# Decode attention on one core: the output projection's weights as one last transfer, and K transposed in double chunks

## Chip, cores, metric

One core of a Trainium2 chip. The metric is the device time of one execution in microseconds (us), median of several runs. All runs that are compared here agree within some tenths of a per cent and count as fast runs. (e6_alone below ran once, so its state is unknown; only its trace is used. A difference under 2% counts as "the same" on record; smaller differences are called real here where the 95% interval excludes 1.)

## The reference

One decode step: attention of 2 batches with 32 heads over a cache of 16384 positions, mixed by a gate with a small MLP.

```python
q = (x @ wq)                                  # 2 x 32 heads x 128
scores = einsum("bhqd,bhkd->bhqk", q, k_cache) * 128 ** -0.5
p = softmax(scores); o = einsum("bhqk,bhkd->bhqd", p, v_cache)
a = o.reshape(B, 1, 32 * 128) @ wo            # wo: 4096 x 1024, bf16, 8.4 MB
b = mlp(B_x)                                  # w1, w2, w3, w4
out = g * a + (1 - g) * b
```

K and V are 537 MB of the 572.5 MB that are read once. Everything else has to hide behind that stream.

## The kernel before

K and V come as 64 tiles of 8.4 MB (two heads of one batch each) into a ring of three buffers; one partition of a tile is a contiguous run of 64 KB. K is transposed on the vector engine in 32x32 blocks, 512 elements at a time. The wo rows come head by head: one transfer of 256 KB per head, 2 KB runs (row `h*128+d` on partition `d`), used by 8 matmuls as soon as that head is finished in both batches.

```python
SLOT = NJ * Dh          # 64 KB a partition; three such buffers
V_SPLIT_LAST = [NJ // 2, NJ // 4, NJ // 8, NJ // 16, NJ // 16]   # last V in five pieces

def load_wo(h):
    t = ...             # [P, D], own small ring
    nc.sync.dma_start(out=t[:], in_=A_wo[h * Dh : (h + 1) * Dh, :])

def qk_stage(i):
    ...
    for m in range(NM):                       # 16
        for wh in range(2):
            T = t_tile([P, CJ, 32], FP32)     # 512 elements a partition
            nc.vector.transpose(out=T[:], in_=Kw[:, m * CJ : (m + 1) * CJ, wh, :])
            ...                               # two matmuls on T into S

def pv_stage(i):
    ...
    (pv_rows if i < NT - 1 else pv_cols)(V, PT, oc)
    nc.vector.tensor_tensor(out=OT[:, hg * G : (hg + 1) * G, b], in0=oc[:], in1=rinv[:], op=ALU.mult)

def wo_stage(h):        # OT: [d, head, batch]
    woh = wo_tiles.pop(h)[:].rearrange("d (p c) -> d p c", c=KC)
    for c in range(KC):
        nc.tensor.matmul(wo_acc[:, c, :], lhsT=woh[:, :, c], rhs=OT[:, h, :], ...)
# ... the transfers and stages are issued in the order k0, k1, v0, k2, v1, o0, ...
```

Of the kernel before, what the change touches and what calls it, by code (L numbers as in the profile page):

```python
# [10 lines left out]
FP32 = mybir.dt.float32  # L11
BF16 = mybir.dt.bfloat16
ACTF = mybir.ActivationFunctionType
ALU = mybir.AluOpType
# [9 lines left out]
def kernel(  # L24
# [17 lines left out]
    B, Sq, D = A_x.shape  # L42
    _, H, Sk, Dh = A_k_cache.shape
    F = B_w3.shape[1]
    assert Sq == 1 and Dh == P and B == 2 and H % 2 == 0
    G = 2
    NJ = G * Sk // P
    CJ = 16
# [11 lines left out]
    const = ctx.enter_context(tc.tile_pool(name="const", bufs=1))  # L60
    big = ctx.enter_context(tc.tile_pool(name="big", bufs=NBIG))
    tpool = ctx.enter_context(tc.tile_pool(name="tpool", bufs=2))
    wpool = ctx.enter_context(tc.tile_pool(name="wpool", bufs=1))
    ppool = ctx.enter_context(tc.tile_pool(name="ppool", bufs=1))
    stat = ctx.enter_context(tc.tile_pool(name="stat", bufs=2))
    sps = ctx.enter_context(tc.tile_pool(name="sps", bufs=2, space=PSUM))
# [7 lines left out]
    def big_tile(name):  # L74
        return big.tile([P, SLOT], BF16, tag="big", name=name)

    def t_tile(shape, dtype, name="T"):
        return tpool.tile(shape, dtype, tag="T", name=name)
# [3 lines left out]
    tiles = [(b, hg) for hg in range(NHG) for b in range(B)]  # L82
    kn_tiles = {}
    vn_tiles = {}
    wo_tiles = {}
    wt = {}
    V_SPLIT_LAST = [NJ // 2, NJ // 4, NJ // 8, NJ // 16, NJ // 16]

    def cache_rows(cache, i):
        b, hg = tiles[i]  # L90
        return cache[b, hg * G : (hg + 1) * G].rearrange("a s d -> (a s) d").rearrange(
            "(p j) d -> p j d", p=P
        )
# [7 lines left out]

    def load_v(i):
        t = big_tile("Vn")
        tv = t[:].rearrange("p (j d) -> p j d", d=Dh)
        src = cache_rows(A_v_cache, i)
        j0 = 0
        for n in V_SPLIT_LAST if i == NT - 1 else [NJ]:
            nc.sync.dma_start(out=tv[:, j0 : j0 + n, :], in_=src[:, j0 : j0 + n, :])
            j0 += n
        vn_tiles[i] = t  # L110

    def load_rows(keys, srcs):
# [7 lines left out]
            wt[key] = v  # L120
            c0 += R * N

    def load_wo(h):
        if h >= H - G:
            t = t_tile([P, D], BF16, "woh")
        else:
            t = wpool.tile([P, D], BF16, tag="woh", name="woh")
        nc.sync.dma_start(out=t[:], in_=A_wo[h * Dh : (h + 1) * Dh, :])
        wo_tiles[h] = t


    x_pm = const.tile([P, B, KC], BF16)
# [55 lines left out]
    for a in range(4):  # L188
        nc.vector.memset(own[32 * a : 32 * a + 32, 2 * a : 2 * a + 2], 1.0)
    ZW = P + NM  # L190
    NZ = 2
    z_tiles = []
    for n in range(NZ):
        z = const.tile([P, 4, ZW], BF16, name=f"z{n}")
# [76 lines left out]
        )  # L271


    OT = const.tile([P, H, B], BF16)
    wo_acc = acc.tile([P, KC, B], FP32, name="wo_acc")
    S_tiles = {}
    PT_tiles = {}
    rs_tiles = {}

    def qk_stage(i):  # L280
        Kw = kn_tiles.pop(i)[:].bitcast(FP32).rearrange("p (j w e) -> p j w e", w=2, e=32)
        z = z_tiles[i % NZ]
        S = sps.tile([P, NC_], FP32, name="S")
        S_tiles[i] = S
        for m in range(NM):
            for wh in range(2):
                T = t_tile([P, CJ, 32], FP32)
                nc.vector.transpose(out=T[:], in_=Kw[:, m * CJ : (m + 1) * CJ, wh, :])  # L288
                Tb = T[:].rearrange("p j s -> p (j s)").bitcast(BF16).rearrange(
                    "p (n two) -> p n two", two=2  # L290
                )
                for par in range(2):
                    nc.tensor.matmul(  # L293
                        S[:],
                        lhsT=z[:, 2 * wh + par, NM - 1 - m : NM - 1 - m + P],
                        rhs=Tb[:, :, par],
                        start=(m == 0 and wh == 0 and par == 0),
                        stop=(m == NM - 1 and wh == 1 and par == 1),
                    )

    def softmax_stage(i):
        S = S_tiles.pop(i)
# [26 lines left out]
    def pv_rows(V, PT, oc):  # L329



        O = ops.tile([P, 4 * Dh], FP32, name="O")
        for m in range(NM):
            for g in range(4):
                j0 = m * CJ + 4 * g
                nc.tensor.matmul(  # L337
                    O[32 * g : 32 * g + 32, :],
                    lhsT=PT[:, m : CJ * 32 : 16],
                    rhs=V[:, j0 : j0 + 4, :],  # L340
                    start=(m == 0),
                    stop=(m == NM - 1),
                )
        Os = ppool.tile([P, 4, Dh], FP32, tag="PrOs", name="Os")
        nc.scalar.copy(out=Os[:].rearrange("p x d -> p (x d)"), in_=O[:])  # L345
        for x in range(4):
            nc.tensor.matmul(  # L347
                oc[:], lhsT=Os[:, x, :], rhs=osel[:, x, :], start=(x == 0), stop=(x == 3)
            )

    def pv_cols(V, PT, oc):
        for j in range(NJ):
            c = (j % CJ) * 32 + j // CJ
            nc.tensor.matmul(  # L354
                oc[:],
                lhsT=V[:, j, :],
                rhs=PT[:, c : c + 17 : 16],
                start=(j == 0),
                stop=(j == NJ - 1),
            )  # L360

    def pv_stage(i):
        b, hg = tiles[i]
        PT = PT_tiles.pop(i)
        rs = rs_tiles.pop(i)
        V = vn_tiles.pop(i)[:].rearrange("p (j d) -> p j d", d=Dh)
        rs2 = stat.tile([P, G], FP32, name="rs2")
        nc.vector.tensor_scalar(
            out=rs2[:], in0=hmask[:], scalar1=rs[:, 0:1], scalar2=None, op0=ALU.mult
        )  # L370
        rinv = stat.tile([P, G], FP32, name="rinv")
        nc.vector.reciprocal(out=rinv[:], in_=total(rs2[:])[:])
        oc = misc_psum([P, G])
        (pv_rows if i < NT - 1 else pv_cols)(V, PT, oc)
        nc.vector.tensor_tensor(  # L375
            out=OT[:, hg * G : (hg + 1) * G, b], in0=oc[:], in1=rinv[:], op=ALU.mult
        )

    def wo_stage(h):

        woh = wo_tiles.pop(h)[:].rearrange("d (p c) -> d p c", c=KC)
        for c in range(KC):
            nc.tensor.matmul(  # L383
                wo_acc[:, c, :],
                lhsT=woh[:, :, c],
                rhs=OT[:, h, :],
                start=(h == 0 and c == 0),
                stop=(h == H - 1 and c == KC - 1),
            )


    def layernorm(src, dst):
# [20 lines left out]
        nc.vector.tensor_tensor(out=dst, in0=cen[:], in1=over_r(rstd[:]), op=ALU.mult)  # L413

    def gelu(pre_f32, dst_bf, C):
        sq = const.tile([P, C, B], FP32, name=f"gelu_sq{C}")
        nc.vector.tensor_tensor(out=sq[:], in0=pre_f32, in1=pre_f32, op=ALU.mult)
        nc.vector.tensor_scalar(
            out=sq[:], in0=sq[:], scalar1=GELU_C1, scalar2=1.0, op0=ALU.mult, op1=ALU.add
        )  # L420
        nc.vector.tensor_tensor(out=sq[:], in0=sq[:], in1=pre_f32, op=ALU.mult)
        nc.scalar.activation(out=sq[:], in_=sq[:], func=ACTF.Tanh, scale=GELU_C0)
        nc.vector.tensor_scalar(
            out=sq[:], in0=sq[:], scalar1=1.0, scalar2=0.5, op0=ALU.add, op1=ALU.mult
        )
        nc.vector.tensor_tensor(out=dst_bf, in0=sq[:], in1=pre_f32, op=ALU.mult)

    def linear(key, actT):

        w = wt.pop(key)  # L430
        R, C = w.shape[1], w.shape[2] // P
        ps = misc_psum([P, C, B])
        for c in range(C):
            for r in range(R):
                nc.tensor.matmul(  # L435
                    ps[:, c, :],
                    lhsT=w[:, r, :].rearrange("k (p c) -> k p c", c=C)[:, :, c],
                    rhs=actT[:, r, :],
                    start=(r == 0),
                    stop=(r == R - 1),  # L440
                )
        return ps
# [3 lines left out]
    shT = const.tile([P, KC, B], BF16)  # L446
    x1 = const.tile([P, KC, B], FP32)
    xn2T = const.tile([P, KC, B], BF16)
    h2 = const.tile([P, FC, B], FP32)
    h2T = const.tile([P, FC, B], BF16)  # L450
    pre = const.tile([P, KC, B], FP32)

# [11 lines left out]
        layernorm(x1[:], xn2T[:])  # L464

    def st_up():
        nc.vector.tensor_copy(out=h2[:], in_=linear("w3", xn2T)[:])
        gelu(h2[:], h2T[:], FC)

# [14 lines left out]
    for i in range(-1, NT):  # L484
        if i + 1 < NT:
            xfers.append(("big", f"k{i + 1}", lambda i=i: load_k(i + 1)))
            steps.append((f"k{i + 1}", lambda i=i: (build_z(i + 1), qk_stage(i + 1))))
        if i >= 0:
            xfers.append(("big", f"v{i}", lambda i=i: load_v(i)))
            steps.append((f"v{i}", lambda i=i: pv_stage(i)))  # L490

            for h in range(max(i - 1, 0), i + (i == NT - 1)) if i else ():
                ring = "wo" if h < H - G else "T"
                xfers.append((ring, f"o{h}", lambda h=h: load_wo(h)))
                steps.append((f"o{h}", lambda h=h: wo_stage(h)))
        if i + 1 < NT:
            steps.append(("", lambda i=i: softmax_stage(i + 1)))
        if i in extra:
            xfers.append(("big", f"x{i}", extra[i][0]))
            steps.append((f"x{i}", extra[i][1]))  # L500

    ring_size = {"big": NBIG, "wo": 1, "T": G}
    ring_used = {"big": [], "wo": [], "T": [f"k{NT - 1}"] * G}
    done = set()

    def issue_ready():
# [54 lines left out]
```

## Time and profile before

| | before |
|---|---|
| time, median of 4 runs | 1350.89 us |
| share of the load queue | 98.7% of 16 DMA engines |
| PE / vector engine (DVE) busy | 68% / 58% |
| last packet of loads ends | 1345.0 us |

These are lines of the page of before: the span, the busy times, two rows of the span in 40 slices (DMA is the busy share of 16 DMA engines in tenths, GB/s what they moved), the queues, and two groups of instructions (busy us, mean ns of one, idle time before them and what ended it).

```profile
span 1349.4 us, 14402 instructions
...
PE 918.6 (68%) x5770; PEld 402.5 (30%) x5770; DVE 786.5 (58%) x1373; ACT 45.0 (3%) x99; POOL 14.3 (1%) x45
...
DMA  9999999999999999999999999999999999999995
GB/s 405 436 436 434 430 432 428 434 430 428 436 423 436 440 427 424 435 441 428 424 440 434 430 426 436 429 429 440 428 428 440 430 426 419 426 422 438 435 418 220
...
q1 hardware_dynamic: 15808, 572.54, 98.7%
...
q14 instruction: 22, 0.18, 0.0%
...
L288 DVE STREAM_TRANSPOSE T<-Kn 128x512 f32<-128x512 f32 x1024 | 691.3, 702 | 231.3 <-DMA Kn<-in_A_k_cache_dram 164.7
...
L383 PE MATMUL wo_acc<-OT,woh 128*128 128x2 bf16 x256 | 20.1, 200 | 4.0 <-DVE OT L375 4.0
```

The DMA row says it all: full until the last slice. The vector engine's 231 us of idle time before its transposes were mostly ended by a K tile that arrived, so it waits for DMA and not the other way round.

The timeline of before at its end (start, length, engine, line, operation, tile, count, idle before):

```profile
1344.82 0.17 DVE L375 TENSOR_TENSOR OT<-misc,rinv 128x2 bf16<-128x2 f32 x1 [6.75 <-PE misc L354]
1344.90 1.21 PEld L383 LDWEIGHTS <-woh 128*128 128x128 bf16 x16 [0.21 <-DMA woh<-in_A_wo_dram]
1345.04 1.16 PE L383 MATMUL wo_acc<-OT,woh 128*128 128x2 bf16 x16 [0.26 <-DVE OT L375]
1346.23 0.17 DVE L524 TENSOR_TENSOR fin<-wo_acc,g_bc 128x16 f32<-128x16 f32 x1 [1.25 <-PE wo_acc L383]
```

The last V product is done at 1344.8 and the last packet of wo ends at 1345.0; 4.4 us after that the kernel is over. There is little to gain at the end other than by ending the stream earlier.

In the records a transfer is a set of packets, here one for each contiguous run: the 8192 packets of 64 KB are 64 tiles of 128 partitions, the 4096 of 2 KB are 32 heads of 128 rows. The records of single DMA packets are in the trace too. They are not on the page; these are sums over them.

```
packet of   count   usual length
64 KB        8192   2.42 us    (27 GB/s for one engine)
 2 KB        4096   0.084 us   (24 GB/s: the wo rows)
```

### The profile page before, as it was taken

To read this page: it belongs to the slowest core of one execution; us is meant where nothing else is said; L and a number is where in the kernel's file an instruction comes from. 1 tells how busy PE (TensorE), PEld (TensorE's weight loads), DVE (VectorE), ACT (ScalarE), POOL (GpSimd) and SP (SyncE) were. 2 spreads that over 40 slices of the span, in tenths; PEclk is the share of its full clock that TensorE was granted. 3 is DMA by queue.
4 is the path that set the end of the run, shared out by engine and by line. 5 is a ranking of instruction groups with operands and counts; after the bars stand their busy time and mean duration, and the time that the engine had idled before them with its cause. 6 is when DMAs were issued, how large, how long until landed. Compare 5 with 4: busy or idle time off the path is not lost.

```text
span 1349.4 us, 14402 instructions
## 1 busy us (share of the span) xinstructions
PE 918.6 (68%) x5770; PEld 402.5 (30%) x5770; DVE 786.5 (58%) x1373; ACT 45.0 (3%) x99; POOL 14.3 (1%) x45
## 2 busy tenths in 40 slices
PE   2677766677667766667766776666876666776667
PEld 2132322432225322223222532222322222332224
DVE  0677765467553655556665365555766555666554
ACT  0000000000000000000000000000000000000000
POOL 0000000000000000000000000000000000000000
PEclk9988878798777777789877787788987778997777
DMA  9999999999999999999999999999999999999995
GB/s 405 436 436 434 430 432 428 434 430 428 436 423 436 440 427 424 435 441 428 424 440 434 430 426 436 429 429 440 428 428 440 430 426 419 426 422 438 435 418 220
DMA packets 15875, 573.46 MB, mean 425 GB/s; under 512 B 2368, under 2 KB 2368, under 8 KB 6720
## 3 DMA queue, kind: packets, MB, share of 16 engines
q1 hardware_dynamic: 15808, 572.54, 98.7%
q8 instruction: 45, 0.74, 0.2%
q14 instruction: 22, 0.18, 0.0%
HBM read 572.53 MB, written 0.00 MB: 424 GB/s over the span
## 4 chain that ended last, share of the span: by engine, by line
DMA 49%; PE 27%; DVE 18%; issue 2%; another core or an unknown queue 2%; ACT 1%; SPq 0%; ACTq 0%
DMA Kn<-in_A_k_cache_dram 49%; PE S L293 19%; DVE T L288 17%; PE O L337 5%; PE misc L347 1%; PE misc L203 1%; PE wo_acc L383 1%; ACT Os L345 1%; PE misc L354 1%; ACT Pr L321 0%; DVE PT L325 0%; DVE mx L314 0%; DVE OT L375 0%; DVE nb L316 0%
## 5 line engine op out<-in xcount | busy, mean ns | idle before, releaser
L288 DVE STREAM_TRANSPOSE T<-Kn 128x512 f32<-128x512 f32 x1024 | 691.3, 702 | 231.3 <-DMA Kn<-in_A_k_cache_dram 164.7
L293 PE MATMUL S<-T,z_133 128*128 128x512 bf16 x1024 | 334.3, 420 | 145.0 <-DVE T L288 133.5
L293 PE MATMUL S<-T,z_135 128*128 128x512 bf16 x1024 | 336.3, 423 | 139.4 <-DVE T L288 124.0
L293 PEld LDWEIGHTS <-z_133 128*128 128x128 bf16 x1024 | 106.7, 104 | 369.8 <-issue 316.1
L293 PEld LDWEIGHTS <-z_135 128*128 128x128 bf16 x1024 | 107.2, 105 | 365.1 <-issue 312.2
L337 PE MATMUL O<-Vn,PT 128*32 128x512 bf16 x1984 | 114.1, 383 | 0.0
L375 DVE TENSOR_TENSOR OT<-misc,rinv 128x2 bf16<-128x2 f32 x32 | 5.2, 163 | 151.4 <-PE misc L347 144.6
L337 PEld LDWEIGHTS <-PT 128*32 128x32 bf16 x1984 | 71.1, 140 | 42.7 <-issue 13.7
L345 ACT COPY Os<-O 128x512 f32<-128x512 f32 x31 | 18.1, 585 | 1099.8 <-PE O L337 1099.8
L347 PE MATMUL misc<-osel,Os 128*128 128x2 f32 x248 | 32.7, 254 | 12.6 <-ACT Os L345 11.1
L435 PEld LDWEIGHTS <-wt 128*128 128x128 bf16 x576 | 35.8, 172 | 16.0 <-DMA wt<-in_B_w_dram 14.7
L325 DVE STREAM_TRANSPOSE PT<-Pr 128x512 bf16<-128x512 bf16 x32 | 22.7, 711 | 28.7 <-ACT Pr L321 28.7
L347 PEld LDWEIGHTS misc<-osel,Os 128*128 128x128 f32 x248 | 30.0, 191 | 21.1 <-ACT Os L345 21.1
L304 DVE TENSOR_REDUCE m<-S 128x1 f32<-128x512 f32 x32 | 22.2, 692 | 22.5 <-PE S L293 22.5
L314 DVE TENSOR_REDUCE mx<-misc 64x1 f32<-64x64 f32 x64 | 14.2, 222 | 23.9 <-PE misc L203 23.5
L321 ACT ACTIVATE Pr<-S,nb 128x512 bf16<-128x512 f32 x32 | 22.0, 687 | 131.0 <-DVE nb L316 128.0
L241 PE MATMUL misc<-xT,wt 128*128 128x2 bf16 x256 | 7.1, 165 | 25.8 <-DVE xT L236 22.9
L383 PEld LDWEIGHTS <-woh 128*128 128x128 bf16 x256 | 20.7, 168 | 10.4 <-issue 10.2
L383 PE MATMUL wo_acc<-OT,woh 128*128 128x2 bf16 x256 | 20.1, 200 | 4.0 <-DVE OT L375 4.0
L203 PE MATMUL misc<-mdiag,ones_f 128*128 128x128 f32 x64 | 16.7, 347 | 8.5 <-DVE mdiag L307 8.5
L435 PE MATMUL misc<-xn2T,wt 128*128 128x2 bf16 x224 | 14.4, 202 | 7.3 <-DMA wt<-in_B_w_dram 7.3
L435 PE MATMUL misc<-h2T,wt 128*128 128x2 bf16 x224 | 13.6, 199 | 7.0 <-DMA wt<-in_B_w_dram 7.0
(173 smaller groups left out, 140.0 us busy)
## 6 DMA issues: line engine op xcount, KB each, us to landing
wt<-in_B_w_dram SPq DMA_DIRECT2D x2, 7168.0 KB, 46.9
woh<-in_A_wo_dram SPq DMA_DIRECT2D x32, 256.0 KB, 30.1
wt<-in_B_w_dram SPq DMA_DIRECT2D x2, 2048.0 KB, 36.4
Vn<-in_A_v_cache_dram SPq DMA_DIRECT2D x1, 4096.0 KB, 38.9
Vn<-in_A_v_cache_dram SPq DMA_DIRECT2D x1, 2048.0 KB, 43.3
Vn<-in_A_v_cache_dram SPq DMA_DIRECT2D x1, 1024.0 KB, 45.2
Vn<-in_A_v_cache_dram SPq DMA_DIRECT2D x2, 512.0 KB, 46.9
Kn<-in_A_k_cache_dram SPq DMA_DIRECT2D x32, 48.9
```

Of the source, the lines that this page charges most:

```text
L203: nc.tensor.matmul(ps[:], lhsT=ones_f[:], rhs=src, start=True, stop=True)
L288: nc.vector.transpose(out=T[:], in_=Kw[:, m * CJ : (m + 1) * CJ, wh, :])
L293: nc.tensor.matmul(S[:], lhsT=z[:, 2 * wh + par, NM - 1 - m : NM - 1 - m + P], rhs=Tb[:, :, par], start=(m == 0 and wh == 0 and par == 0), ...
L304: nc.vector.reduce_max(out=m[:], in_=S[:], axis=AX.X)
L314: nc.vector.reduce_max(out=mx[pa, :], in_=mall[pa, pa], axis=AX.X)
L321: nc.scalar.activation(out=Pr[:], in_=S[:], func=ACTF.Exp, bias=nb[:], scale=scale, accum_out=rs[:])
L325: nc.vector.transpose(out=PT[:], in_=Pr[:])
L337: nc.tensor.matmul(O[32 * g : 32 * g + 32, :], lhsT=PT[:, m : CJ * 32 : 16], rhs=V[:, j0 : j0 + 4, :], start=(m == 0), stop=(m == NM - 1),)
L345: nc.scalar.copy(out=Os[:].rearrange("p x d -> p (x d)"), in_=O[:])
L347: nc.tensor.matmul(oc[:], lhsT=Os[:, x, :], rhs=osel[:, x, :], start=(x == 0), stop=(x == 3))
L383: nc.tensor.matmul(wo_acc[:, c, :], lhsT=woh[:, :, c], rhs=OT[:, h, :], start=(h == 0 and c == 0), stop=(h == H - 1 and c == KC - 1),)
L435: nc.tensor.matmul(ps[:, c, :], lhsT=w[:, r, :].rearrange("k (p c) -> k p c", c=C)[:, :, c], rhs=actT[:, r, :], start=(r == 0), stop=(r == ...
```

## The change

Intent: read wo in long runs instead of 2 KB, without small transfers between the K and V tiles, and spend fewer vector instructions on K. After the last V, wo comes as one transfer into a big buffer, in six pieces of 16, 8, 4, 2, 1, 1 rows a partition. Partition `32a+h` gets rows `h*128 + 32a + r`, r = 0..31, a contiguous 64 KB. That is the order in which one transpose of 32x32 blocks puts the head outputs. To make room, one z tile goes, and some small tiles move into the ring of T.

```diff
-    V_SPLIT_LAST = [NJ // 2, NJ // 4, NJ // 8, NJ // 16, NJ // 16]      # last V now whole, by rows
-    def load_wo(h): ...
+    WO_SPLIT = [16, 8, 4, 2, 1, 1]
+    def load_wo():
+        t = big_tile("wo")[:].rearrange("p (r n) -> p r n", n=D)
+        src = A_wo.rearrange("(h a r) n -> a h r n", a=4, r=32)
+        r0 = 0
+        for n in WO_SPLIT:
+            nc.sync.dma_start(out=t[:, r0 : r0 + n, :], in_=src[:, :, r0 : r0 + n, :])
+            r0 += n
 ...
-    NZ = 2
+    NZ = 1
 ...  # qk_stage: one transpose of [P, 2, CJ, 32] (1024 elements) and four matmuls, 16 times a tile
+            T = t_tile([P, 2, CJ, 32], FP32)
 ...
-    def wo_stage(h): ...
+    def wo_stage():
+        Q = const.tile([P, B, 32], BF16)
+        for b in range(B):
+            nc.vector.transpose(out=Q[:, b, :], in_=OT[:, b, :])     # OT: [d, batch, head]
+        wo = wt.pop("wo").rearrange("k r (p c) -> k r p c", c=KC)
+        for r in range(32):
+            for c in range(KC):
+                nc.tensor.matmul(wo_acc[:, c, :], lhsT=wo[:, r, :, c], rhs=Q[:, :, r], ...)
 ...
+    xfers.append(("big", "wo", load_wo)); steps.append(("wo", wo_stage))
```

More of the change, by code (lines that the diff above doesn't have):

```diff
@@ L44 @@
     F = B_w3.shape[1]
-    assert Sq == 1 and Dh == P and B == 2 and H % 2 == 0
+    assert Sq == 1 and Dh == P and B == 2 and H == 32
     G = 2
@@ L62 @@
     tpool = ctx.enter_context(tc.tile_pool(name="tpool", bufs=2))
-    wpool = ctx.enter_context(tc.tile_pool(name="wpool", bufs=1))
     ppool = ctx.enter_context(tc.tile_pool(name="ppool", bufs=1))
@@ L84 @@
     vn_tiles = {}
-    wo_tiles = {}
     wt = {}
-    V_SPLIT_LAST = [NJ // 2, NJ // 4, NJ // 8, NJ // 16, NJ // 16]
     def cache_rows(cache, i):
@@ L103, in load_v @@
         t = big_tile("Vn")
-        tv = t[:].rearrange("p (j d) -> p j d", d=Dh)
-        src = cache_rows(A_v_cache, i)
-        j0 = 0
-        for n in V_SPLIT_LAST if i == NT - 1 else [NJ]:
-            nc.sync.dma_start(out=tv[:, j0 : j0 + n, :], in_=src[:, j0 : j0 + n, :])
-            j0 += n
+        nc.sync.dma_start(
+            out=t[:].rearrange("p (j d) -> p j d", d=Dh), in_=cache_rows(A_v_cache, i)
+        )
         vn_tiles[i] = t
@@ L121, in load_rows @@
             c0 += R * N
-    def load_wo(h):
-        if h >= H - G:
-            t = t_tile([P, D], BF16, "woh")
-        else:
-            t = wpool.tile([P, D], BF16, tag="woh", name="woh")
-        nc.sync.dma_start(out=t[:], in_=A_wo[h * Dh : (h + 1) * Dh, :])
-        wo_tiles[h] = t
+    WO_SPLIT = [16, 8, 4, 2, 1, 1]
[6 more added lines that the diff above has]
+            r0 += n
+        wt["wo"] = t
     x_pm = const.tile([P, B, KC], BF16)
@@ L271, in build_z @@
         )
-    OT = const.tile([P, H, B], BF16)
+    OT = const.tile([P, B, H], BF16)
     wo_acc = acc.tile([P, KC, B], FP32, name="wo_acc")
@@ L280, in qk_stage @@
     def qk_stage(i):
-        Kw = kn_tiles.pop(i)[:].bitcast(FP32).rearrange("p (j w e) -> p j w e", w=2, e=32)
+        Kw = kn_tiles.pop(i)[:].bitcast(FP32)
         z = z_tiles[i % NZ]
@@ L284, in qk_stage @@
         S_tiles[i] = S
+        CW = CJ * Dh // 2
         for m in range(NM):
-            for wh in range(2):
-                T = t_tile([P, CJ, 32], FP32)
-                nc.vector.transpose(out=T[:], in_=Kw[:, m * CJ : (m + 1) * CJ, wh, :])
-                Tb = T[:].rearrange("p j s -> p (j s)").bitcast(BF16).rearrange(
-                    "p (n two) -> p n two", two=2
-                )
-                for par in range(2):
-                    nc.tensor.matmul(
-                        S[:],
-                        lhsT=z[:, 2 * wh + par, NM - 1 - m : NM - 1 - m + P],
-                        rhs=Tb[:, :, par],
-                        start=(m == 0 and wh == 0 and par == 0),
-                        stop=(m == NM - 1 and wh == 1 and par == 1),
-                    )
+            T = t_tile([P, 2, CJ, 32], FP32)
+            nc.vector.transpose(
+                out=T[:].rearrange("p w j s -> p j w s"),
+                in_=Kw[:, m * CW : (m + 1) * CW].rearrange("p (j w e) -> p j w e", w=2, e=32),
+            )
+            Tb = T[:].rearrange("p w j s -> p w (j s)").bitcast(BF16).rearrange(
+                "p w (n two) -> p w n two", two=2
+            )
+            for v in range(4):
+                nc.tensor.matmul(
+                    S[:],
+                    lhsT=z[:, v, NM - 1 - m : NM - 1 - m + P],
+                    rhs=Tb[:, v // 2, :, v % 2],
+                    start=(m == 0 and v == 0),
+                    stop=(m == NM - 1 and v == 3),
+                )
     def softmax_stage(i):
@@ L349, in pv_rows @@
             )
-    def pv_cols(V, PT, oc):
-        for j in range(NJ):
-            c = (j % CJ) * 32 + j // CJ
-            nc.tensor.matmul(
-                oc[:],
-                lhsT=V[:, j, :],
-                rhs=PT[:, c : c + 17 : 16],
-                start=(j == 0),
-                stop=(j == NJ - 1),
-            )
     def pv_stage(i):
@@ L373, in pv_stage @@
         oc = misc_psum([P, G])
-        (pv_rows if i < NT - 1 else pv_cols)(V, PT, oc)
+        pv_rows(V, PT, oc)
         nc.vector.tensor_tensor(
-            out=OT[:, hg * G : (hg + 1) * G, b], in0=oc[:], in1=rinv[:], op=ALU.mult
+            out=OT[:, b, hg * G : (hg + 1) * G], in0=oc[:], in1=rinv[:], op=ALU.mult
         )
-    def wo_stage(h):
-        woh = wo_tiles.pop(h)[:].rearrange("d (p c) -> d p c", c=KC)
-        for c in range(KC):
-            nc.tensor.matmul(
-                wo_acc[:, c, :],
-                lhsT=woh[:, :, c],
-                rhs=OT[:, h, :],
-                start=(h == 0 and c == 0),
-                stop=(h == H - 1 and c == KC - 1),
-            )
+    def wo_stage():
[5 more added lines that the diff above has]
+            for c in range(KC):
+                nc.tensor.matmul(
+                    wo_acc[:, c, :],
+                    lhsT=wo[:, r, :, c],
+                    rhs=Q[:, :, r],
+                    start=(r == 0 and c == 0),
+                    stop=(r == 31 and c == KC - 1),
+                )
     def layernorm(src, dst):
@@ L415, in gelu @@
     def gelu(pre_f32, dst_bf, C):
-        sq = const.tile([P, C, B], FP32, name=f"gelu_sq{C}")
+        sq = t_tile([P, C, B], FP32, "gelu")
         nc.vector.tensor_tensor(out=sq[:], in0=pre_f32, in1=pre_f32, op=ALU.mult)
@@ L448 @@
     xn2T = const.tile([P, KC, B], BF16)
-    h2 = const.tile([P, FC, B], FP32)
     h2T = const.tile([P, FC, B], BF16)
@@ L466, in st_up @@
     def st_up():
+        h2 = t_tile([P, FC, B], FP32, "h2")
         nc.vector.tensor_copy(out=h2[:], in_=linear("w3", xn2T)[:])
@@ L490 @@
             steps.append((f"v{i}", lambda i=i: pv_stage(i)))
-            for h in range(max(i - 1, 0), i + (i == NT - 1)) if i else ():
-                ring = "wo" if h < H - G else "T"
-                xfers.append((ring, f"o{h}", lambda h=h: load_wo(h)))
-                steps.append((f"o{h}", lambda h=h: wo_stage(h)))
         if i + 1 < NT:
@@ L500 @@
             steps.append((f"x{i}", extra[i][1]))
-    ring_size = {"big": NBIG, "wo": 1, "T": G}
-    ring_used = {"big": [], "wo": [], "T": [f"k{NT - 1}"] * G}
+    xfers.append(("big", "wo", load_wo))
+    steps.append(("wo", wo_stage))
+    ring_size = {"big": NBIG}
+    ring_used = {"big": []}
     done = set()
```

## The prediction

> **What bounds the kernel now.** DMA. The queue table gives the load queue 98.7% of 16 engines' span; PE is 68% and DVE 58% busy (page). In the packet records of the trace the last load packet ends 1345.0 us after the span's start; 4.4 us remain (16 matmuls, two DVE operations, the store). Most engines end at 1330 to 1336 us, two at 1343 and 1345. K's work is off the path: DVE waits 5.8 us for the last K tile (chain of waits).
>
> **Removed.**
> - 32 transfers of 256 KB in 2 KB packets. A 2 KB packet takes 84 ns, a 64 KB one 2420 (packet records): 21.8 us of all 16 engines for wo, against an estimated 19.7 in the new runs (32 KB 1215 ns, 16 KB 613, 8 KB 309, 4 KB 159, 2 KB 84). About 2 us, on the path.
> - 512 transposes' fixed cost. 702 ns for 512 elements is about 0.53 us of elements and 0.17 fixed (my split), so 1.24 us for a double chunk instead of 1.40: 85 us less DVE time, worth nothing under a DMA limit.
> - The last V tile's 256 column matmuls (6.9 us, timeline) become rows (3.6 us).
>
> **Added or moved.**
> - All 256 wo matmuls stand at the end, 63 ns each as in the first projection (64 in 3.96 us): 16 us. If wo landed at full rate, PE would end about 6 us behind the last piece, and the time would be about 1353 us.
> - The new transfer's source is 4 blocks, then 32 heads, then a contiguous run; the two outer strides cannot merge, so the slowest dimension is 4. [...] The trace of before has no such transfer to check it. If it holds, 8.4 MB go through 4 engines: 32 partitions x 2.46 us = 79 us (estimate from the packet times above) instead of 20.
>
> **Sum.** Without wo ahead of it, each engine ends V 22 us earlier: most at 1308 to 1313 us, the late two at 1320 to 1323. The wo transfer waits for the last K tile, done at about 1304, so it is queued by then. Plus 79: 1387 to 1392, or up to 1402 if a late engine is among the four. Plus 3.9 of tail and 1.5 between span and timed run: 1393 to 1407. I say 1398 us, range 1386 to 1411. If all 16 engines work, 1348 to 1356.
> Chances: faster by over 2% 0.01, within 2% 0.21, slower 0.78.
>
> **What would show it.** The last two slices at a quarter DMA share and about 108 GB/s; the chain of waits ending in wo transfers; wo pieces landing some 39, 20, 10, 5 us apart; 2 KB packets down from 4096 to 256; 512 transposes at 1.2 to 1.25 us. With 16 engines: wo lands 20 us after V, then 5 to 6 us of matmuls.
>
> **What would make it wrong.** The lowering splits the dimension, or spreading follows partitions, so that 16 engines work; four engines alone exceed 27 GB/s each; the single z buffer starves the queue, which I do not expect.

"If it holds" refers to the premise that the new transfer, with a slowest dimension of 4, runs on four engines. The result shows that it did (a DMA share of 0.25, four reports of landing a piece). 1308 to 1323 for the end of V, plus 79 for wo on four engines, plus 3.9 and 1.5, came to 1393 to 1407, and the prediction said 1398. The 79 us are an estimate that needs the premise; the packet times in it are medians in before (32 KB 1.215 us, 16 KB 0.613, 8 KB 0.312, 4 KB 0.160, 2 KB 0.084). The split of a transpose was an estimate too; the two sizes measured, 702 ns in before and 1229 in after, give 527 ns for 512 elements and 175 fixed, taken as linear.

## The result

| | before | after |
|---|---|---|
| time, median of 4 runs | 1350.89 us | 1420.08 us |
| ratio (95% interval) | | 1.051 (1.049 to 1.053) |

A ratio is the mean time of one kernel's fast runs over that of the other's of the same rounds, so it is not quite the ratio of the medians. The result is correct, and the change is 5% slower. The prediction had the direction and said 1398 (1386 to 1411); the time lies 9 us above the range.

The page of after, the same lines:

```profile
span 1417.6 us, 12917 instructions
...
PE 827.6 (58%) x5523; PEld 400.9 (28%) x5586; DVE 707.6 (50%) x862; ACT 45.5 (3%) x100; POOL 14.4 (1%) x45
...
DMA  9999999999999999999999999999999999999221
GB/s 413 439 423 435 439 428 429 437 426 441 428 432 432 429 438 433 424 441 437 419 443 435 424 435 435 432 432 431 439 430 429 435 437 422 441 433 394 85 89 58
...
q1 hardware_dynamic: 11416, 572.54, 93.9%
...
q14 instruction: 14, 0.11, 0.0%
...
L286 DVE STREAM_TRANSPOSE T<-Kn 128x1024 f32<-128x1024 f32 x512 | 612.2, 1229 | 266.8 <-DMA Kn<-in_A_k_cache_dram 218.3
...
L378 PE MATMUL wo_acc<-Q,wo 128*128 128x2 bf16 x256 | 16.4, 199 | 73.7 <-DMA wo<-in_A_wo_dram 73.7
```

Up to slice 36 of 40 nothing is lost. The last three slices, 106 us, move almost nothing but wo: a quarter of the DMA engines' time and less, 58 to 89 GB/s. PE waited 73.7 us for wo inside its own 256 matmuls. The stretches of after (us, busy time and count of PE, PEld, DVE, ACT, POOL, granted PE clock, DMA share, GB/s) put a number on it:

```profile
1260.00:1300.00 40.00, 24.84 (x170) 11.53 (x168) 21.81 (x25) 1.36 (x3) 0.00 (x0) 0.83 1.01 435
1316.00:1346.00 30.00, 6.70 (x72) 3.44 (x72) 0.37 (x2) 0.58 (x1) 0.00 (x0) 0.61 0.25 84
1346.00:1376.00 30.00, 3.30 (x55) 3.30 (x56) 0.00 (x0) 0.00 (x0) 0.00 (x0) 0.50 0.25 88
```

A share of 0.25 for 60 us is four engines at work, and the trace says it directly: each wo piece has four reports of landing that follow its data, where a transfer on all engines has 16. Four engines at the 27 GB/s that a 64 KB packet shows would move 108 GB/s; they moved 84 to 88. So there are two findings: only four engines, and some of them slow. The packet records show which: for the first piece, two of the four engines took 1.22 us a packet from 1316 us on, and two took up to 2.4 us. The four landed it at 1346.5, 1355.8, 1371.0 and 1372.7 us, and the first matmul on it began at 1372.70.

The chain of waits of after has a trap (start, length, what):

```profile
1297.53 15.46 SPq L125
...
1313.03 54.90 SPq L125
...
1367.98 21.85 SPq L125
...
1389.87 23.89 DMA wo<-in_A_wo_dram
...
1413.81 0.66 PE wo_acc L378 x8
```

It puts most of the end down to the queue SPq, that is, to issuing wo transfers: issuing the fourth piece alone took 54.9 us. That looks like a limit of the issue. The packet records say otherwise; the last packet of each size of wo ended at:

```
piece (rows)  run     last packet ends   after the one before   32 packets at their usual length
16            32 KB   1372.1 us          68.0 (from 1304.1)     38.9
8             16 KB   1393.0             21.0                   19.6
4              8 KB   1403.0              9.9                    9.9
2              4 KB   1408.0              5.0                    5.1
1 and 1        2 KB   1413.3              5.3                    5.4
```

The slowest engine went from piece to piece without a pause, so the issue was not what it waited for. What held up the issue was not shown; in e2_perm below, where 16 engines share the same number of wo packets, all six pieces were issued in 2.7 us. Of the 109 us of wo, the first piece has 29 us more than its packets need, and the other four rows add up to 41 against 40. Of the 128 packets of 32 KB, half took over 1.4 us and a quarter 2.4 us, which is twice the usual 1.215.

The sum of the result: wo 1304.1 to 1413.3, then 4.3 us to the end of the span, then 2.5 us between the span and the median of the runs.

### The profile page after: what moved, and what is told of

Its sections match the earlier page's. It is cut to its first block, busy times and chain, and to the rows that moved or that the text cites. A ratio compares the mean times of both kernels' runs of the same rounds, so it can differ in the third digit from the quotient of the medians.

```text
span 1417.6 us, 12917 instructions
## 1 busy us (share of the span) xinstructions
PE 827.6 (58%) x5523; PEld 400.9 (28%) x5586; DVE 707.6 (50%) x862; ACT 45.5 (3%) x100; POOL 14.4 (1%) x45
## 4 chain that ended last, share of the span: by engine, by line
PE 25%; DVE 21%; DMA 21%; another core or an unknown queue 12%; issue 11%; SPq 7%; ACT 2%; ACTq 0%; POOL 0%
DVE T L286 18%; DMA Kn<-in_A_k_cache_dram 16%; PE S L294 13%; SPq L125 7%; PE O L338 6%; DMA wt<-in_B_w_dram 4%; PE misc L430 3%; PE misc L201 2%; PE misc L348 2%; DMA wo<-in_A_wo_dram 2%; ACT Pr L322 1%; DVE PT L326 1%; ACT Os L346 1%; DVE mx L315 1%
## 5 line engine op out<-in xcount | busy, mean ns | idle before, releaser
L294 PE MATMUL S<-T,z 128*128 128x512 bf16 x1985 | 581.3, 421 | 342.3 <-DVE T L286 321.7
L286 DVE STREAM_TRANSPOSE T<-Kn 128x1024 f32<-128x1024 f32 x512 | 612.2, 1229 | 266.8 <-DMA Kn<-in_A_k_cache_dram 218.3
L294 PEld LDWEIGHTS <-z 128*128 128x128 bf16 x2048 | 218.7, 107 | 699.4 <-issue 537.2
L338 PE MATMUL O<-Vn,PT 128*32 128x512 bf16 x2048 | 119.8, 387 | 10.2 <-DMA Vn<-in_A_v_cache_dram 10.2
L201 PE MATMUL misc<-rs,ones_f 128*128 128x2 f32 x64 | 17.9, 350 | 76.5 <-DVE rs L358 76.5
L378 PE MATMUL wo_acc<-Q,wo 128*128 128x2 bf16 x256 | 16.4, 199 | 73.7 <-DMA wo<-in_A_wo_dram 73.7
L201 PEld LDWEIGHTS misc<-rs,ones_f 128*128 128x128 f32 x64 | 16.2, 314 | 81.2 <-issue 78.5
L378 PEld LDWEIGHTS <-wo 128*128 128x128 bf16 x256 | 15.9, 169 | 74.2 <-DMA wo<-in_A_wo_dram 74.2
L264 POOL TENSOR_TENSOR z<-qsel,own 128x32 bf16<-128x32 bf16 x32 | 10.8, 337 | 1225.6 <-PE S L294 1194.6
```

What stands on the lines that cost most here:

```text
L201: nc.tensor.matmul(ps[:], lhsT=ones_f[:], rhs=src, start=True, stop=True)
L286: nc.vector.transpose(out=T[:].rearrange("p w j s -> p j w s"), in_=Kw[:, m * CW : (m + 1) * CW].rearrange("p (j w e) -> p j w e", w=2, e=32),
L294: nc.tensor.matmul(S[:], lhsT=z[:, v, NM - 1 - m : NM - 1 - m + P], rhs=Tb[:, v // 2, :, v % 2], start=(m == 0 and v == 0), stop=(m == NM ...
L338: nc.tensor.matmul(O[32 * g : 32 * g + 32, :], lhsT=PT[:, m : CJ * 32 : 16], rhs=V[:, j0 : j0 + 4, :], start=(m == 0), stop=(m == NM - 1),)
L378: nc.tensor.matmul(wo_acc[:, c, :], lhsT=wo[:, r, :, c], rhs=Q[:, :, r], start=(r == 0 and c == 0), stop=(r == 31 and c == KC - 1),)
```

## Experiments

Two questions: do four engines explain the stretch, or is it wo at the end as such? And what doubles the time of many packets? The theory for the first was the prediction's premise: the number of engines follows the slowest dimension of the transfer, 4 in after. For the second it was a guess about the destination: two engines that write partitions 32 apart at the same time hold each other up. In after, if each engine takes one block (the records don't name the engines), engine a fills partitions 32a to 32a+31, so neighbours write 32 apart. Up to here only the four engines of after are measured; e1_blocks, e2_perm and e6_alone test the rest. Rivals: the source addresses collide, or a lone engine is slower.

### e1_blocks: the same layout, one transfer per block

```diff
-            nc.sync.dma_start(out=t[:, r0 : r0 + n, :], in_=src[:, :, r0 : r0 + n, :])
+            for a in range(4):
+                nc.sync.dma_start(out=t[32 * a : 32 * a + 32, r0 : r0 + n, :], in_=src[a, :, r0 : r0 + n, :])
```

> The changed kernel with each of the six wo pieces cut into four transfers, one per block of 32 partitions, so that the slowest dimension of both sides is 32. Engine-count theory [...]: all 16 engines carry wo and the long stretch at a quarter DMA share goes. Under it two sizes: if two engines [...] halve each other, wo still takes about twice the 20 us of a full-rate transfer, span about 1363 to 1372 us; if engines do not disturb each other, wo takes 20 us and the 256 matmuls trail by about 6 us, span about 1350 to 1354. Rival (the new last transfer costs because it waits for the K slot, because the matmuls are all at the end, or because the DMA issue blocks): stays at 1400 or more.

Measured: 1365.1 us, ratio to before 1.010 (1.009 to 1.012). The layout in SBUF is the same; the slowest dimension went from 4 to 32 and the transfers from 6 to 24, and 55 us of the 69 lost are back. The two DMA rows of its page:

```profile
DMA  9999999999999999999999999999999999999995
GB/s 400 435 448 429 429 431 424 434 437 435 429 437 431 431 433 439 431 429 429 429 429 441 439 431 429 433 429 433 439 431 429 431 433 431 437 441 430 431 253 141
```

In the last slice but one nine tenths of all engines' time is busy, yet they move 253 GB/s. The packets of 32 KB took 2.47 us on average. From 1316 to 1340 us the DMA share was 0.85, against 0.25 in after. So the engine count was the larger part, and the doubling remains: 2.47 us against the usual 1.215, in transfers that each fill 32 partitions. What makes 16 engines on 32 partitions slow was not shown.

### e2_perm: one dimension of 128

```diff
-        src = A_wo.rearrange("(h a r) n -> a h r n", a=4, r=32)
+        src = A_wo.rearrange("(p r) n -> p r n", p=P)          # partition 4h+a
...
+        qp = misc_psum([P, B, 32])                             # bring Q into that order
+        nc.tensor.matmul(qp[:], lhsT=perm[:].rearrange("p h a -> p (h a)"), rhs=Q[:], start=True, stop=True)
+        nc.vector.tensor_copy(out=Q[:], in_=qp[:])
```

`perm` is a 128x128 matrix of zeros and ones, `perm[32a+h, 4h+a] = 1`.

> The changed kernel with the wo rows laid over the partitions in plain order (partition 4h+a, one dimension of 128), and one extra matmul with a permutation matrix that brings the head outputs into that order; result correct. Engine-count theory: 16 engines[...], wo lands 20 us after V, matmuls trail by about 6 us: time 1350 to 1356 us. Rival (end-loading of wo itself costs the 70 us): over 1400.

Measured: 1345.73 us, 0.996 of before (0.995 to 0.997), result correct. That is below the expected 1350 to 1356: the rival falls, and something else had been gained that nobody had counted. The packets of 32 KB took 1.217 us on average.

### e6_alone: the transfers by themselves

A kernel of twelve transfers, each into the same tile, so each waits for the one before (wrong result).

```python
blocks = A_wo.rearrange("(h a r) n -> a h (r n)", a=4, r=32)
plain = A_wo.rearrange("(p r) n -> p (r n)", p=P)
far = spaced(2, 64)                          # rows of 32 KB from the K cache, 96 KB apart
for rep in range(2):
    load("plain128", 0, 128, plain[:, 0:N])              # N = 16 * 1024
    load("wo4x32", 0, 128, blocks[:, :, 0:N])
    load("kc4x32", 0, 128, spaced(4, 32))                # blocks 3.2 MB apart
    load("kc2x32", 0, 64, far[:, 0:32, :])
    load("kc2x64", 0, 128, far)
    load("wo32", 0, 32, blocks[0, :, 0:N])
```

> Wrong result on purpose: only transfers, one at a time into the same tile, 32 KB runs, each twice. (1) plain, 128 rows to 128 partitions; (2) wo as in the change, 4 blocks of 32; (3) 4 blocks of 32 from the K cache, blocks 3.2 MB apart instead of 64 KB; (4) 2 blocks of 32 to partitions 0 to 63; (5) 2 blocks of 64 to partitions 0 to 127; (6) 32 rows to 32 partitions. Destination theory (two engines that write partitions 32 apart[...] at the same time halve each other): packets of (1) 1.22 us, of (2), (3), (4) about 2.4 us in lockstep, so (2) and (3) land after about 75 us and (4) after about 75; (5) 64 packets of 1.22 us per engine, also about 78 us; (6) 2 packets of 2.4 us. Source theory (the blocks' addresses 64 KB apart collide): (2) slow, (3) to (6) at 1.22 us a packet, so (3) and (4) land after about 40 us. Lone-engine theory (few engines are slower each): 2.4 us in (5) too.

Five stretches of e6_alone, each inside one transfer of the first round, in the order wo4x32, kc4x32, kc2x32, kc2x64, wo32 (us, DVE, POOL, clock, DMA share, GB/s):

```profile
16.00:88.00 72.00, 0.00 (x0) 0.00 (x0) 1.00 0.24 56
93.00:168.00 75.00, 0.00 (x0) 0.00 (x0) 1.00 0.24 54
172.00:243.00 71.00, 0.00 (x0) 0.00 (x0) 1.00 0.12 29
247.00:321.00 74.00, 0.00 (x0) 0.00 (x0) 1.00 0.12 54
324.00:330.00 6.00, 0.00 (x0) 0.00 (x0) 1.00 0.82 175
```

The shares are 4/16, 4/16, 2/16 and 2/16: with 4 blocks in the source four engines worked, with 2 blocks two. The reports of landing agree: 4, 4, 2, 2, and 16 for the 32 rows of wo32. The third and the fourth line are the pair to look at. Both have two engines and the same kind of source; the third writes partitions 0 to 31 and 32 to 63, the fourth 0 to 63 and 64 to 127. The third moves 29 GB/s, the fourth 54, which is 27 an engine. So few engines are not slow as such, and the destination decides. The first two lines have sources that differ (blocks 64 KB and 3.2 MB apart) and the same destination, and they agree: the source is not it. Packets of 32 KB had medians of 2.42 and 2.45 us in lines one and two, 2.41 in line three, 1.21 in line four. The plain transfer of 4 MB landed in 12.0 us and that of 1 MB to 32 partitions in 7.2. While the latter ran it moved 175 GB/s at a share of 0.82, about 13 an engine. The numbers of the destination theory hold for all six; partitions 32 apart explain the second to the fifth, not the sixth.

### e3_kold: is it the K chunk?

The gain in e2_perm that had not been counted had to be somewhere. e3_kold is e2_perm with the K stage of before.

```diff
-            T = t_tile([P, 2, CJ, 32], FP32)     # 512 transposes of 1024
+            for wh in range(2): T = t_tile([P, CJ, 32], FP32) ...   # 1024 transposes of 512
```

> The same as e2_perm, with the K stage of before (1024 transposes of 512 elements, 702 ns each) in place of 512 of 1024 elements (1229 ns). If the K chunk is off the path as predicted: within 1 us of e2_perm. If the longer chunk has a cost or a gain on the path: apart by 2 us or more.

Measured: 1353.97 us, 1.002 of before (1.001 to 1.004). The K chunk is worth 8.2 us, though the vector engine has time to spare. The prediction's view of it is refuted. The repaired wo part alone costs 3.1 us against before.

A first hint is in the landings. A transfer's 16 engines report one by one: for the last V of after from 1304.6 to 1316.9 us, and its matmuls began at 1316.97. In the last wo piece of e3_kold, one engine lands 9.3 us after the next to last; in e2_perm it is 1.4 us. In before, one engine is late too, by 9.2 us. The first matmul on wo in after also began with the last of four reports (1372.7 us), 26 us after the first, so one late engine can set the pace for all. The queue lines of e3_kold and then of e2_perm show what differs:

```profile
q1 hardware_dynamic: 11488, 572.54, 98.3%
...
q14 instruction: 22, 0.18, 0.0%
```

```profile
q1 hardware_dynamic: 11488, 572.54, 98.7%
...
q14 instruction: 14, 0.11, 0.0%
```

Eight fewer packets on the queue of instructions (fetches, from here on; 8 KB each), with the same loads. With semaphore waits counted, the vector engine has 2374 instructions in e3_kold and 1350 in e2_perm. Two theories: fetching vector instructions takes time from one DMA engine; or the shorter chunk gives the K buffers back later.

### e8_slow and e7_tiny, e7b_tiny: instructions or time?

```diff
+        red = stat.tile([P, 1], FP32, name="red")                       # e8_slow: once a K tile
+        nc.vector.reduce_max(out=red[:], in_=Kw[:, 0:2560], axis=AX.X)
```

> e2_perm with one reduction over 2560 elements of K at the end of each K stage: 32 more instructions, about 2.7 us more vector time per K tile, and the K slot is given back later by as much, as with the short chunk. Instruction-count theory: 1345 to 1347 us, as e2_perm. Slot theory: 1352 to 1355 us, as e3_kold.

Measured: 1346.11 us, 0.996 (0.995 to 0.998). Vector time is added (the reduction took 2.78 us a K tile; 788.6 us busy, about as much as before) and hardly any instructions (32): no change. The slot theory falls.

```diff
+            for _ in range(2):                                          # e7_tiny: after each transpose
+                nc.vector.memset(tiny[:], 0.0)
```

> e2_perm with two memsets of one element per partition after each transpose: 1024 more vector instructions, about 2 us more vector time per K tile. The K chunk was worth 8 us in e2_perm against e3_kold although the vector engine is off the path. Instruction-count theory (each fetch of vector instructions takes time from a DMA engine that is the slowest one, and the longer chunk saves about 1000 instructions): 1351 to 1355 us, and the last engine lands several us behind the next as in e3_kold. Slot theory (the vector engine gives K slots back later): about 1345.7 plus nothing to 2, if the added time does not matter there, and the same as e8_slow.

Measured: 1376.7 us, 1.019 (1.018 to 1.020). This tells nothing. The memsets (59 ns each, 1.9 us a K tile) depend on nothing, and the scheduler moved them to the front. DMA dropped to seven tenths in slices 5 to 7, and in the middle of the run the timeline has six transposes in a row without a memset between them. (It had 21 fetches, and yet its last engine was only 0.1 us behind at the end. Nine of the 21 came before 240 us, against 2 of 14 in e2_perm: the added ones belong to the early stretch in which the queue ran dry, where the delay of one engine was made up for (its lag there fell from 2.4 us to nothing); so it is no test of the next point either way.)

```diff
-                nc.vector.memset(tiny[:], 0.0)
+                nc.vector.tensor_copy(out=tiny[:], in_=T[:, 0, 0, 0:1])  # e7b_tiny
```

> e7_tiny done again: its memsets depended on nothing and the scheduler moved them to the front, where they held up the start, so that it told nothing. Here two copies of one element per partition out of the freshly transposed chunk follow each transpose, so they stay in place; the vector engine then has 2374 instructions, as many as e3_kold, against 1350 in e2_perm. Instruction-count theory: 1351 to 1356 us, and one DMA engine lands several us after the next, as in e3_kold and before. If the number of instructions is not the cause: 1345 to 1348 us.

Measured: 1350.25 us, 0.999 (0.998 to 1.001). The expected count of instructions was too high: there are 1957 and not 2374 (the reading is that waits which had been instructions of their own now ride on the copies). The time lies just under the range given for 2374 and well above that for no effect. It fits by proportion:

| kernel | vector instructions | fetches on q14 | last engine behind the next, last wo piece | time |
|---|---|---|---|---|
| e2_perm | 1350 | 14 | 1.4 us | 1345.7 us |
| e8_slow | 1382 | 14 | 1.6 us | 1346.1 us |
| e7b_tiny | 1957 | 18 | 5.2 us | 1350.3 us |
| e3_kold | 2374 | 22 | 9.3 us | 1354.0 us |

From e2_perm to e7b_tiny it is 4.5 us for 607 instructions, to e3_kold 8.2 us for 1024: 7.4 and 8.0 ns each, or about 1 us a fetch. The number of instructions, not their time, is what cost here, and the fetches went with it, 14, 14, 18 and 22. The packet records tie this to the fetches, although they don't name the engine of a packet. In e3_kold, 19 of the 22 fetches, of 8 KB and about 0.33 us, begin just as a packet of the loads ends, and just as they end a 64 KB packet begins that takes 2.8 to 3.1 us in place of 2.42 (all within 0.03 us; in e7b_tiny it is 18 of 18, in e2_perm 13 of 14). Of all 64 KB packets in e3_kold only 1.4% are that slow. By these times a fetch held one engine for 0.33 us, and the packet after it took about 0.6 us longer: together the 1 us. The lag of the last engine also grows step by step in e3_kold, mostly by 0.9 us at a fetch: 0.5 us after 2 fetches, 5.1 after 12, 9.3 after 22. It falls back at times, when the next engine has lost time as well. Why the packet after a fetch is slower stays open.

### e9_after_kold: the wo part of the change alone

The changed kernel with the K stage of before (the diff of e3_kold).

> The changed kernel with the K stage of before: the wo part of the change alone. Prediction's view (the K chunk is off the path): 1418 to 1422, as the change. If the late DMA engine that the short chunk makes is one of the four that carry wo: 1426 to 1430.

Measured: 1440.03 us, 1.066 (1.064 to 1.067). Both expectations are missed: the K chunk is worth 20 us here. The first wo packet starts about 6 us later, the first piece takes about 9 us longer still (mean packet of 32 KB 1.81 us against 1.67), and the other pieces take about 6 us longer, also with slower packets (16 KB: 0.74 us against 0.64). As in after, three engines began wo together (1310.0 to 1310.4 us) and the fourth 12 us later; in both runs two engines, which began together, were slow, and the other two, far apart in time, were not. The slow two took about 2.4 us a packet of 32 KB on average here, against about 2.1 in after, so by the packet times they were in step for longer. What decides how long two engines stay in step was not tested.

### e4_tail: the end of e2_perm

The timeline of e2_perm's end (columns as before):

```profile
1315.59 5.86 PE L345 MATMUL O<-Vn,PT 128*32 128x512 bf16 x64 [8.10 <-DMA Vn<-in_A_v_cache_dram]
...
1325.38 15.54 PE L390 MATMUL wo_acc<-Q,wo 128*128 128x2 bf16 x256 [1.48 <-DMA wo<-in_A_wo_dram]
1340.96 0.17 DVE L529 TENSOR_TENSOR fin<-wo_acc,g_bc 128x16 f32<-128x16 f32 x1 [16.80 <-PE wo_acc L390]
```

The 256 matmuls run without a pause from 1325.4 to 1340.9, while the last wo piece has landed at 1335.2. They start late and end 5.7 us behind, as the prediction had it for 16 engines.

```diff
-    WO_SPLIT = [16, 8, 4, 2, 1, 1]
+    WO_SPLIT = [4] * 6 + [2, 2, 2, 1, 1]
-        pv_rows(V, PT, oc)
+        (pv_rows if i < NT - 1 else pv_cols)(V, PT, oc)      # and the last V in five pieces, as before
```

> e2_perm with two things for its end: the last V again in five pieces and multiplied by columns as before, and wo in eleven pieces (six of 4 rows, then 2, 2, 2, 1, 1) in place of six. In e2_perm the wo matmuls (0.5 us a row) start late because half of wo is one piece and the V product ends some 6 us after V, so they end about 5.6 us after the last landing. If that is so, they now keep up with the landings (0.61 us a row) and the time falls by 4 to 5 us, to 1341 to 1342. If the trail has another cause (the matmuls slow down beside the transfer, or start late for another reason), it stays at 1345 to 1346.

Measured: 1342.23 us, 0.9935 of before (0.992 to 0.995), result correct: faster than both kernels, if only by 0.65% of before. The expected cause holds: in its timeline the groups of 32 matmuls (4 rows) take 2.10 us each, start every 2.48 us (0.62 us a row) and wait 0.4 us for the next piece, and the last ones end about 1 us after the last piece has landed.

```profile
1328.05 2.10 PE L404 MATMUL wo_acc<-Q,wo 128*128 128x2 bf16 x32 [0.38 <-DMA wo<-in_A_wo_dram]
...
1330.53 5.95 PE L404 MATMUL wo_acc<-Q,wo 128*128 128x2 bf16 x96 [0.38 <-DMA wo<-in_A_wo_dram]
1336.51 0.17 DVE L543 TENSOR_TENSOR fin<-wo_acc,g_bc 128x16 f32<-128x16 f32 x1 [19.33 <-PE wo_acc L404]
```

## Why the prediction was right, and where it failed

**DMA is the limit: right.** Every kernel that reads all data on 16 engines at full rate lies within 1342 to 1354 us, but for e7_tiny, which held up its own start.

**Four engines: right.** It was a premise that no trace of before showed. After shows a share of 0.25 and four reports of landing a piece, e6_alone 0.24 and 0.12 for 4 and 2 blocks, and e1_blocks and e2_perm bring 55 and 74 us back by changing the dimension.

**"32 partitions x 2.46 us = 79 us": wrong, and this is the step that failed.** wo took 109 us. The term used the packet times of before, where 16 engines fill 128 partitions and a packet of 32 KB took 1.215 us. In after the first piece took 68 us in place of 39, because two of the four engines were in step and their packets took up to twice as long; the other two, which began 11.5 us apart, took 41.0 and 38.8 us. That the pair in step wrote partitions 32 apart is the guess from the layout, as the records don't name the engines; that such a destination halves two engines is shown by e6_alone, with the destination as the only difference (29 against 54 GB/s). The prediction thought of four engines being faster than 27 GB/s each, and not of their being slower. The later pieces hardly suffered: 41 us against 40.

**Where the sum stood otherwise.** The prediction had the four engines start wo at 1308 to 1323 and end at 1387 to 1402. Three started at 1304.1 to 1305.0 and the fourth at 1316.5, and wo ended at 1413.3. So 30 us more in wo were offset in part by the earlier start, and 22 us remain between 1398 and 1420. The prediction also read two late engines in before (1343 and 1345); the packets and landings there show one, at 1345. Its lag grows with the fetches in before as well, to 9.2 us over 22 of them.

**The K chunk "worth nothing under a DMA limit": wrong.** The size of one transpose was right (1.24 us predicted, 1.229 measured), and so was the view that the vector engine's time doesn't matter (e8_slow). But 1024 fewer vector instructions were worth 8.2 us in e3_kold against e2_perm, and 20 us in the changed kernel. Without that the change would have been at 1440 (e9_after_kold), so it is luck that two errors partly cancelled and the miss is 22 us and not 42.

**Long runs, "about 2 us": fits.** e3_kold has the wo part with 16 engines, the old K chunk and as many fetches as before. Its last wo packet lands at 1343.5 us against 1345.5, so the stream ends 2.0 us earlier; its matmuls end 5.7 us after that landing against 0.7. The difference, 3 us, is what it is slower than before. Other small things differ too (the last V is one piece), so the 2 us are not shown to be the runs' alone.

**The single z buffer: right** as far as seen. In after the matmuls of K had 0.4 us of idle time that ended with z.

**What would show it.** Pieces 39, 20, 10, 5 us apart came as 68, 21, 10, 5; 108 GB/s came as 84 to 88; 256 packets of 2 KB and 512 transposes came as said.

## What to carry to other kernels

Look at the slowest dimension of a transfer before anything else. Here a source of 4 blocks ran on four engines and cost 74 us against one of 128 rows, and one small permutation matmul in the kernel was enough to do without the blocks (1420.1 against 1345.7 us). If engines do end up on blocks of partitions, ask which of them write partitions 32 apart at the same moment: in e6_alone two engines on blocks 32 apart moved 29 GB/s, on blocks 64 apart 54. And where DMA limits for the whole length, as here, count the vector instructions too: here each cost 7.4 to 8.0 ns of the kernel's time, so a longer instruction on an engine with time to spare was worth more than its busy time says.
